# 480 guest columns of wq instead of 240, brought by SP and GpSimd

## The chip, the cores and the metric

The kernel runs on one core of one Trainium2 chip. The metric is device time in microseconds (us): the median of several runs of the whole program.

## The reference

One decode step (one token, batch 4) of a transformer block with adaptive layer norm: sliding window attention over a cache, then a gated feed-forward layer. All is float32.

```python
mod = (silu(c) @ w_mod).reshape(B, 6, 1, -1)           # sa, ca, ga, sb, cb, gb
h = layernorm(x) * (1 + ca) + sa                       # x: [4, 1, 512]
q = h @ wq                                             # wq: 512 x 4096, 32 heads of 128
# keys and values: the last 2048 positions of the cache, 8 heads, each shared by 4 query heads
o = softmax(q k^T / sqrt(128)) v
x = x + ga * (o @ wo)
h = layernorm(x) * (1 + cb) + sb
x = x + gb * ((silu(h @ w1) * (h @ w3)) @ w2)          # w1, w3: 512 x 1792, w2: 1792 x 512
```

## The kernel before

About 101 MB of weights, keys and values are loaded once, and nearly every load has 128 partitions, so that its rows are spread evenly over the 16 DMA engines. The big buffer `ring` has three `slots` of 16384 columns (64 KB a partition). `w_mod_a` (the modulation weights for sa and ca, with x and c) lands in the first 4128 columns of `slots[0]`, `wq` in `slots[1]`, and the cache of the eight groups (`kv[0]` to `kv[7]`, one per key head) goes round the slots: `kv[0]` in `slots[2]`, `kv[1]` in `slots[0]` when the modulation columns no longer need it, `kv[2]` in `slots[1]` when the queries no longer need wq, and so on. Later come `wo_mod`, `last_k_wo`, `last_v`, `wo`, `w1`, `w3` and `w2` (in four pieces). SP issues all loads but wq, which ACT issues.

Instructions are recorded by `do(engine, method, ...)` in program order (all of them at one source line, L59, in the profile). `Program` works out which earlier accesses overlap, and puts semaphore waits in front of an instruction; each engine and each queue goes through its own instructions in the order written. A wait on an engine is a wait for the latest of its instructions that touches the same place.

The start: `w_mod_a` and `wq` are loaded; constants are made on GpSimd (POOL in the profile) and VectorE (DVE); then layer norm, `mod_columns` (the modulation columns on TensorE, PE), `modulate`, which gives `h`, and `transposed`, which gives `hT`. Then the queries: wq is laid out so that `s_ps[half]` takes half of the heads; its four quarters of 32 partitions (i = 0 to 3) each sum four products (k = 0 to 3) of 512 columns. The loops are half, k, i, with i innermost.

**Guests.** The last 240 columns of wq's last quarter (half 1, i = 3, k = 3) aren't in the load of wq. Their 128 rows lie in another input, `guests`, 24 rows of 6 x 240 columns, and come by eight loads of SP, each of 3 partitions (4 apart), to the partitions 0 to 11 and 32 to 43 of `p_all`, over zeros. The matching rows of h come from six matmuls of `h` with a slice of the identity (`hp`, copied to `hg`), and six matmuls with `hg` and `guest` add the guests' share to the last 240 columns of the quarter.

Behind the queries come, for each group g, the scores, the softmax, the products with the values and the heads (`group`), and after `group(g)` the issue of `kv[g + 3]`. The end is the feed-forward layer, whose last pieces of w2 arrive last.

Of the kernel before, what the change touches and what calls it, by code (L numbers as in the profile page):

```python
# [11 lines left out]
NT = 4  # L12
# [1 line left out]
CHUNKS = [(c, j) for c in range(4) for j in range(4 if c < 2 else 3)]  # L14
NF = len(CHUNKS)
W2_CUTS = [0, 8, 11, 13, 14]
GUESTS = 240
GUEST_AT = [(0, 0, 12), (12, 0, 12), (24, 0, 8), (64, 0, 12), (76, 0, 12), (84, 4, 12)]
EPS = 1e-5
HALF = 8192  # L20

# [123 lines left out]
                nc.sync.sem_clear(done)  # L145


def block_kernel(nc, w_mod_a, wq, guests, kv_in, wo_mod, last_k_wo, last_v, wo, w1, w3, w2, out):

# [2 lines left out]
    do = Program(nc)  # L154

    def sb(name, *shape):
        return nc.alloc_sbuf_tensor(name, (P, *shape), F32).ap()
# [5 lines left out]
    slots = [ring[:, n * 2 * HALF : (n + 1) * 2 * HALF] for n in range(3)]  # L163
# [6 lines left out]
    def bank():  # L170
        turn[0] += 1
        return banks[turn[0] % 2]

    def load(dst, src, cuts=(0, 1), queue="sync"):
        step = src.shape[1] // cuts[-1]
        for lo, hi in zip(cuts[:-1], cuts[1:]):
            do(queue, "dma_start", dst[:, lo * step : hi * step], src[:, lo * step : hi * step])
        return dst[:, : src.shape[1]]
# [9 lines left out]
    wq_t = load(slots[1], wq, queue="scalar")  # L188
    do("scalar", "preload_act_table_set", "natural_log_exp_and_others")
    kv = [None] * G  # L190
# [4 lines left out]
    ident = shifted[:, 4:]  # L195
    do("gpsimd", "memset", shifted, 0.0)
    do("gpsimd", "affine_select", ident, ident, compare_op=ALU.not_equal, fill=1.0, base=0, pattern=[[-1, P]], channel_multiplier=1)

    p_all = sb("p_sb", NT * 512)
    do("gpsimd", "memset", p_all[:44], 0.0)  # L200
    guest = p_all[:44, : 6 * GUESTS]
    for m in range(2):
        for c in range(4):
            do("sync", "dma_start", guest[32 * m + c : 32 * m + 12 : 4], guests[12 * m + c : 12 * m + 12 : 4])
    kv[0] = load(slots[2], kv_in[0])
    sc = sb("sc", 4, 32)
    do("gpsimd", "memset", sc, 0.0)
# [11 lines left out]
    spread = sb("spread", 32)  # L219
# [19 lines left out]
    e = sb("e", 16)  # L239
# [5 lines left out]
    xc, sq, h = (sb(n, P) for n in ("xc", "sq", "h"))  # L245
    ss, ln, r0, ve, a, r = (sb(n, 1) for n in ("ss", "ln", "r0", "ve", "a", "r"))
# [19 lines left out]
    def transposed(name):  # L266
        hp = bank()[:, :P]
        do("tensor", "transpose", hp, h, ident)
        hT = sb(name, 4, 32)
        do("vector", "tensor_copy", hT.rearrange("p j i -> p (j i)"), hp)  # L270
        return hT
# [21 lines left out]
    do("vector", "tensor_scalar_add", mod_a[:, P:], mod_a[:, P:], 1.0)  # L293
    modulate(mod_a[:, P:], mod_a[:, :P])
    hT = transposed("hT")
    kv[1] = load(slots[0], kv_in[1])


    hg = p_all[:44, 6 * GUESTS :][:, : 6 * 32]
    hp = bank()[:44, : 6 * 32]  # L300
    for n, (at, _, _) in enumerate(GUEST_AT):
        do("tensor", "matmul", hp[:, 32 * n : 32 * n + 32], h[:, at : at + 44], ident[:, 96:], start=True, stop=True)
    do("vector", "tensor_copy", hg, hp)

    work = sb("work", 512)
    for half in range(2):
        qp = s_ps[half]
        for k in range(4):
            for i in range(4):
                at = ((half * 4 + i) * 4 + k) * 512  # L310
                n = min(512, 16384 - GUESTS - at)
                if n < 512:
                    for c in range(6):
                        do("tensor", "matmul", qp[96:, n:], hg[:, 32 * c : 32 * c + 32], guest[:, c * GUESTS : (c + 1) * GUESTS], start=False, stop=False)
                do("tensor", "matmul", qp[32 * i : 32 * i + 32, :n], hT[:, k, :], wq_t[:, at : at + n], start=(k == 0), stop=(k == 3))
    for half in range(2):
        do("scalar", "mul", work, s_ps[half], DH**-0.5)
        qtp = bank()
# [2 lines left out]
        for i in range(R):  # L321
            src = qtp[:, i * P : (i + 1) * P].rearrange("p (g q) -> p g q", g=4)[:, :, ::8]
# [13 lines left out]
    p_sb = [p_all[:, t * 512 : (t + 1) * 512] for t in range(NT)]  # L336
# [132 lines left out]
    for n in range(W2_CUTS[1]):  # L469
        i = n % 4  # L470
# [22 lines left out]
def _layout(i):  # L493
    import numpy as np

    def a(t):
        return np.ascontiguousarray(t)

    k = i["A_k_cache"][:, :, SK - W :, :].reshape(B, G, NT, 512, DH)
    v = i["A_v_cache"][:, :, SK - W :, :].reshape(B, G, NT, NC, P, DH)  # L500
    wm = i["w_mod"].reshape(4, P, 6, 4, P)
    xc = np.concatenate([i[n].reshape(B, 4, P).transpose(2, 1, 0).reshape(P, 16) for n in ("A_x", "c")], 1)
    w2 = i["B_w2"].reshape(14, P, D)
    wq = a(i["A_wq"].reshape(4, P, G, 512).transpose(1, 2, 0, 3)).reshape(P, 16384)
    guests = np.zeros((2, 12, 6, GUESTS), np.float32)
    for n, (at, lo, hi) in enumerate(GUEST_AT):
        for m in range(2):
            guests[m, lo:hi, n] = wq[at + 32 * m + lo : at + 32 * m + hi, 16384 - GUESTS :]
    wo = a(i["A_wo"].reshape(2, 4, R, P, D).transpose(0, 3, 1, 2, 4)).reshape(2, P, 8192)
    kv = np.concatenate([k.transpose(1, 4, 2, 0, 3).reshape(G, P, 8192), v.transpose(1, 4, 2, 0, 3, 5).reshape(G, P, 8192)], 2)  # L510
    return {
        "w_mod_a": np.concatenate([a(wm[:, :, :2].transpose(1, 0, 3, 2, 4)).reshape(P, 4096), xc], 1),
        "wq": a(wq[:, : 16384 - GUESTS]),
        "guests": guests.reshape(24, 6 * GUESTS),
        "kv_in": kv[: G - 1],
        "wo_mod": np.concatenate([wo[0], a(wm[:, :, 2:].transpose(1, 0, 3, 2, 4)).reshape(P, 8192)], 1),
        "last_k_wo": np.concatenate([kv[G - 1, :, :8192], wo[1, :, :4096]], 1),
        "last_v": a(kv[G - 1, :, 8192:]),
        "wo": a(wo[1, :, 4096:]),
        "w1": a(i["B_w1"].reshape(4, P, FF).transpose(1, 0, 2)).reshape(P, 4 * FF),  # L520
        "w3": a(i["B_w3"].reshape(4, P, FF).transpose(1, 0, 2)).reshape(P, 4 * FF),
        "w2": a(np.stack([w2[4 * j + c] for c, j in CHUNKS], 1)).reshape(P, NF * D),
    }
# [15 lines left out]
```

## Time and profile before

| | |
|---|---|
| runs | 242.0 us median of 3 (241.97 to 242.18) |
| profiled execution | span 240.8 us from the first to the last instruction; the page gives no other time for it |
| busy | PE 148.7 us (62%), weight loads 54.2 (22%), DVE 56.3 (23%), ACT 24.1 (10%), POOL 4.5 (2%) |
| DMA | 101.39 MB in 2937 packets, mean 421 GB/s |
| granted clock of TensorE | 0.865 on average |

The page shows one execution. Its queues q1 and q10 are those of SP and ACT, q8 and q14 fetch instructions. A view in windows gives busy time, granted clock, the mean busy share of the 16 DMA engines and GB/s for chosen stretches; a packet is counted by its start, so that a share in a short stretch can be over 1. The chain is the work that ended last, followed back from the last instruction.

### The profile page before, as it was taken

The numbers are of one execution on the slowest core, as the hardware profiler recorded it, in microseconds if no ns is written. First come the engines' busy times: TensorE is split into PE (matmuls) and PEld (weight loads), VectorE is DVE, ScalarE is ACT, GpSimd is POOL, SyncE is SP. The second block draws the span as 40 slices with busy tenths as digits, with TensorE's granted clock in tenths as the row PEclk, the third lists the DMA queues.
The fourth block names the chain that finished last, engine by engine and source line by source line (L and its number), as shares of the span: only waits on it lengthen the run. The fifth ranks groups of instructions, "written<-read, shape, count | busy, mean of one in ns | idle before, by whom it ended". The sixth has DMA issues, their size and how long they took to land.

```text
span 240.8 us, 2502 instructions
## 1 busy us (share of the span) xinstructions
PE 148.7 (62%) x1113; PEld 54.2 (22%) x1113; DVE 56.3 (23%) x141; ACT 24.1 (10%) x36; POOL 4.5 (2%) x12
## 2 busy tenths in 40 slices
PE   0000169982984962944867576667399719965876
PEld 0000133322322212201312222221042202422333
DVE  5000231034152024123132133130313104113210
ACT  2000000003003003001100300300200001320100
POOL 7000000000000000000000000000000000000000
PEclk9999997997696798879797799795759968995899
DMA  8999999999999999999999999999999999999994
GB/s 305 434 444 455 424 425 446 416 446 414 457 395 468 403 459 414 449 425 446 425 446 427 435 435 435 435 427 446 425 446 425 411 419 430 386 444 443 401 413 162
DMA packets 2937, 101.39 MB, mean 421 GB/s; under 512 B 472, under 2 KB 472, under 8 KB 880
## 3 DMA queue, kind: packets, MB, share of 16 engines
q1 hardware_dynamic: 2784, 92.99, 89.8%
q10 hardware_dynamic: 144, 8.27, 8.0%
q8 instruction: 8, 0.13, 0.2%
q14 instruction: 1, 0.01, 0.0%
HBM read 101.22 MB, written 0.03 MB: 420 GB/s over the span
## 4 chain that ended last, share of the span: by engine, by line
DMA 60%; PE 31%; DVE 5%; ACT 3%; issue 1%; ACTq 0%
DMA ring<-kv_in 33%; DMA ring<-w 16%; PE s_ps L59 14%; DMA ring<-w_mod_a 11%; PE bank L59 9%; PE o_ps L59 6%; DVE nm L59 3%; ACT p_sb L59 3%; PE a_ps L59 1%; DVE mod_a L59 0%; ACT work L59 0%; DVE p_sb L59 0%; DVE e L59 0%; DVE h L59 0%; DVE sq L59 0%
## 5 line engine op out<-in xcount | busy, mean ns | idle before, releaser
L59 PE MATMUL s_ps<-ring,qT 128*32 128x512 f32 x256 | 36.5, 722 | 20.3 <-DMA ring<-kv_in 13.3
L59 PE MATMUL bank<-ident,p_sb 128*128 128x128 f32 (+1 forms) x136 | 27.7, 353 | 30.8 <-ACT p_sb L59 30.7
L59 PE MATMUL o_ps<-ring,pT 128*16 128x512 f32 x256 | 38.4, 707 | 0.1
L59 PEld LDWEIGHTS bank<-ident,p_sb 128*128 128x128 f32 (+1 forms) x136 | 19.8, 178 | 52.5 <-ACT p_sb L59 31.7
L59 ACT ACTIVATE p_sb<-s_ps,nm 128x2048 f32<-128x2048 f32 (+1 forms) x11 | 16.5, 1501 | 139.7 <-DVE oT L59 104.1
L59 DVE TENSOR_REDUCE nm<-s_ps 128x1 f32<-128x2048 f32 x7 | 16.0, 2292 | 32.5 <-PE s_ps L59 32.5
L59 DVE COPY pT<-bank 128x64 f32<-128x64 f32 x32 | 7.2, 225 | 57.0 <-PE bank L59 57.0
L59 PEld LDWEIGHTS s_ps<-ring,qT 128*32 128x32 f32 x256 | 8.7, 129 | 46.9 <-issue 20.1
L59 PE MATMUL bank<-ident,xs 128*128 128x128 f32 x1 | 0.5, 476 | 27.8 <-POOL xs L59 27.8
L59 PE MATMUL s_ps<-ring,h2T 128*32 128x512 f32 (+1 forms) x64 | 9.0, 657 | 2.3 <-DMA ring<-w 2.3
L59 PE MATMUL s_ps<-ring,hT 128*32 128x512 f32 (+1 forms) x64 | 9.4, 705 | 0.0
L59 PEld LDWEIGHTS o_ps<-ring,pT 128*16 128x16 f32 x256 | 5.4, 99 | 11.9 <-issue 9.0
L59 DVE SCALAR_TENSOR_TENSOR o_own<-o_ps,rl,own 128x512 f32<-128x512 f32 x7 | 5.3, 751 | 11.1 <-PE o_ps L59 11.1
L59 PE MATMUL a_ps<-ring,oT 128*4 128x512 f32 x64 | 7.4, 592 | 0.0
L59 DVE TENSOR_REDUCE o_sum<-o_own 128x128 f32<-128x512 f32 x7 | 7.2, 1034 | 0.2
L59 PE MATMUL bank<-ring,sc 128*32 128x256 f32 (+1 forms) x64 | 6.9, 587 | 0.0
L59 PEld LDWEIGHTS bank<-ident,xs 128*128 128x128 f32 x1 | 0.2, 183 | 27.8 <-POOL xs L59 27.8
L59 DVE TENSOR_SCALAR e<-e 128x16 f32<-128x16 f32 x1 | 0.2, 175 | 23.3 <-ACT e L59 23.3
L59 DVE COPY qT<-bank 128x64 f32<-128x64 f32 x8 | 2.2, 280 | 12.4 <-PE bank L59 12.0
L59 DVE TENSOR_REDUCE mx<-s_ps 128x1 f32<-128x512 f32 x4 | 2.8, 692 | 9.0 <-PE s_ps L59 9.0
L59 PEld LDWEIGHTS s_ps<-ring,h2T 128*32 128x32 f32 x64 | 2.6, 130 | 7.3 <-issue 4.4
L59 PE MATMUL s_ps<-ring,hidT 128*32 128x64 f32 (+1 forms) x112 | 3.6, 274 | 0.3 <-DVE hidT L59 0.3
(97 smaller groups left out, 63.7 us busy)
## 6 DMA issues: line engine op xcount, KB each, us to landing
ring<-wq ACTq DMA_DIRECT2D x1, 8072.0 KB, 26.9
ring<-w SPq DMA_DIRECT2D x2, 3584.0 KB, 37.9
ring<-last_k_wo SPq DMA_DIRECT2D x1, 6144.0 KB, 30.1
ring<-last_v SPq DMA_DIRECT2D x1, 4096.0 KB, 39.5
ring<-w_mod_a SPq DMA_DIRECT2D x1, 2064.0 KB, 26.7
ring<-wo SPq DMA_DIRECT2D x1, 2048.0 KB, 41.8
ring<-w SPq DMA_DIRECT2D x1, 2048.0 KB, 43.1
ring<-w SPq DMA_DIRECT2D x1, 768.0 KB, 44.5
```

The source lines that it names most:

```text
L59: op = Op(engine, lambda: getattr(getattr(self.nc, engine), method)(*args, **kw), [])
```

## The change

- `GUESTS` is 480. wq's load is 240 columns narrower still, and the quarter's last product (k = 3) keeps 32 of its 512 columns in it.
- The guests lie on 76 partitions: 0 to 11 and 64 to 75, with zeros between. Their place is `slots[0]`, columns 4128 to 7008, behind `w_mod_a`. VectorE clears it (GpSimd cleared `p_all` before).
- They come in three loads whose two sides are shaped differently. `low`: 12 partitions of 2880 columns, issued by SP; its source has 3 rows of 4 runs. `high_a`: 4 partitions of 3 x 640 columns, from 3 rows of 4 runs, and `high_b`: 8 partitions of 2400 columns, from 2 rows of 4 runs, both issued by GpSimd. In front of these two GpSimd issues a small load of 8 x 2 x 8 elements of wq into `work`, which nothing reads.
- `hg` takes seven matmuls of up to 76 rows (six of 44 before) and two copies (one before).
- The queries are computed quarter by quarter: first half 1, i = 3, with the guests' six matmuls directly behind k = 0; then the other seven quarters, with k innermost.
- The issue of `kv[1]` stands behind that first quarter; before, it stood behind `hT`.

```diff
-GUESTS = 240
-GUEST_AT = [(0, 0, 12), (12, 0, 12), (24, 0, 8), (64, 0, 12), (76, 0, 12), (84, 4, 12)]
+GUESTS = 480
+GUEST_ROWS = 76
+LOW = [[(0, 12, 12 * n)] for n in range(5)] + [[(8, 12, 116), (0, 8, 60)]]
+HIGH = [(64 + 4 * (n == 0), 76, 12 * n) for n in range(5)]
...
-    p_all = sb("p_sb", NT * 512)
-    do("gpsimd", "memset", p_all[:44], 0.0)
-    guest = p_all[:44, : 6 * GUESTS]
-    for m in range(2):
-        for c in range(4):
-            do("sync", "dma_start", guest[32 * m + c : 32 * m + 12 : 4], guests[12 * m + c : 12 * m + 12 : 4])
+    guest = slots[0][:GUEST_ROWS, 4128 : 4128 + 6 * GUESTS]
+    do("vector", "memset", guest, 0.0)
+
+    def quads(queue, dst, src, runs):
+
+        step = dst.shape[-1]
+        src = src[:, : runs * step + runs * 16].rearrange("e (r n) -> e r n", r=runs)[:, :, :step]
+        do(queue, "dma_start", dst, src)
+
+    p_all, work = sb("p_sb", NT * 512), sb("work", 512)
+    quads("sync", guest[:12], low, 4)
+    do("gpsimd", "dma_start", work[:8, :32].rearrange("p (s n) -> p s n", s=2)[:, :, :8], wq[:8, :16].rearrange("p (s n) -> p s n", s=2))
+    quads("gpsimd", guest[64:68, GUESTS : 5 * GUESTS].rearrange("p (a n) -> p a n", a=3), high_a, 4)
+    quads("gpsimd", guest[68:, : 5 * GUESTS], high_b, 4)
     kv[0] = load(slots[2], kv_in[0])
...
     hT = transposed("hT")
-    kv[1] = load(slots[0], kv_in[1])
...
+    tall = [GUEST_ROWS] * 5 + [12]
+    for n, parts in enumerate(LOW):
+        for _, rows, at in parts:
+            rows = GUEST_ROWS if n < 5 else rows
+            do("tensor", "matmul", hp[:rows, 32 * n : 32 * n + 32], h[:, at : at + rows], ident[:, 96:], start=True, stop=True)
+    do("vector", "tensor_copy", hg[:, :160], hp[:, :160])
+    do("vector", "tensor_copy", hg[:12, 160:], hp[:12, 160:])
+
+    def queries(half, i, guests=False):
         qp = s_ps[half]
         for k in range(4):
...
+            at = ((half * 4 + i) * 4 + k) * 512
+            n = min(512, 16384 - GUESTS - at)
+            do("tensor", "matmul", qp[32 * i : 32 * i + 32, :n], hT[:, k, :], wq_t[:, at : at + n], start=(k == 0), stop=(k == 3))
+            if guests and k == 0:
+                for c in range(6):
+                    do("tensor", "matmul", qp[96:, 512 - GUESTS :], hg[: tall[c], 32 * c : 32 * c + 32], guest[: tall[c], c * GUESTS : (c + 1) * GUESTS], start=False, stop=False)
+
+    queries(1, 3, True)
+    kv[1] = load(slots[0], kv_in[1])
+    for half in range(2):
+        for i in range(4 - half):
+            queries(half, i)
...
+    def spread(rows, engines, runs):
+        apart = np.zeros((engines, runs, rows.size // engines // runs + 16), np.float32)
+        apart[:, :, :-16] = rows.reshape(engines, runs, -1)
+        return np.pad(apart.reshape(engines, -1), ((0, 0), (0, 16)))
...
+        "low": spread(guests[:12], 3, 4),
+        "high_a": spread(guests[64:68, GUESTS : 5 * GUESTS], 3, 4),
+        "high_b": spread(guests[68:, : 5 * GUESTS], 2, 4),
```

More of the change, by code (lines that the diff above doesn't have):

```diff
@@ L145, in emit, with block_kernel @@
                 nc.sync.sem_clear(done)
-def block_kernel(nc, w_mod_a, wq, guests, kv_in, wo_mod, last_k_wo, last_v, wo, w1, w3, w2, out):
+def block_kernel(nc, w_mod_a, wq, low, high_a, high_b, kv_in, wo_mod, last_k_wo, last_v, wo, w1, w3, w2, out):
     do = Program(nc)
@@ L295, in block_kernel @@
     hT = transposed("hT")
-    kv[1] = load(slots[0], kv_in[1])
[L299 to L306, printed above, removed]
+    hg = p_all[:GUEST_ROWS, : 6 * 32]
+    hp = bank()[:GUEST_ROWS, : 6 * 32]
+    tall = [GUEST_ROWS] * 5 + [12]
[6 more added lines that the diff above has]
+    def queries(half, i, guests=False):
         qp = s_ps[half]
         for k in range(4):
[L309 to L315, printed above, removed]
+            at = ((half * 4 + i) * 4 + k) * 512
[9 more added lines that the diff above has]
+            queries(half, i)
     for half in range(2):
@@ L504, in _layout @@
     wq = a(i["A_wq"].reshape(4, P, G, 512).transpose(1, 2, 0, 3)).reshape(P, 16384)
[L505 to L508, printed above, removed]
+    guests = np.zeros((GUEST_ROWS, 6, GUESTS), np.float32)
+    for n, parts in enumerate(LOW):
+        for lo, hi, at in parts + HIGH[n : n + 1]:
+            guests[lo:hi, n] = wq[at + lo : at + hi, 16384 - GUESTS :]
+    guests = guests.reshape(GUEST_ROWS, 6 * GUESTS)
+    def spread(rows, engines, runs):
+        apart = np.zeros((engines, runs, rows.size // engines // runs + 16), np.float32)
+        apart[:, :, :-16] = rows.reshape(engines, runs, -1)
+        return np.pad(apart.reshape(engines, -1), ((0, 0), (0, 16)))
     wo = a(i["A_wo"].reshape(2, 4, R, P, D).transpose(0, 3, 1, 2, 4)).reshape(2, P, 8192)
@@ L513, in _layout @@
         "wq": a(wq[:, : 16384 - GUESTS]),
-        "guests": guests.reshape(24, 6 * GUESTS),
+        "low": spread(guests[:12], 3, 4),
+        "high_a": spread(guests[64:68, GUESTS : 5 * GUESTS], 3, 4),
+        "high_b": spread(guests[68:, : 5 * GUESTS], 2, 4),
         "kv_in": kv[: G - 1],
```

## The prediction

> **What bounds the kernel now.** I read the page's head, its queues and chain first.
>
> ```profile
> span 240.8 us, 2502 instructions
> q1 hardware_dynamic: 2784, 92.99, 89.8%
> q10 hardware_dynamic: 144, 8.27, 8.0%
> q8 instruction: 8, 0.13, 0.2%
> DMA 60%; PE 31%; DVE 5%; ACT 3%; issue 1%; ACTq 0%
> ```
>
> SP's and ACT's queues keep the 16 DMA engines busy for 97.8% of the span. PE's 31% of the chain lies beside transfers, save for the end. The time is therefore the time of the DMA engine that finishes last, plus the tail behind it. Next, stretches of the windows view (columns: stretch, its length, PE busy, clock, DMA share, GB/s):
>
> ```profile
> 33.50:36.90 3.40, 1.54 (x29) 1.00 1.29 559
> 36.90:40.30 3.40, 3.40 (x20) 0.50 0.84 366
> 40.30:45.40 5.10, 5.10 (x50) 1.00 0.97 414
> 67.40:190.00 122.60, 83.87 (x554) 0.83 1.00 433
> 236.10:236.40 0.30, 0.30 (x8) 1.00 0.76 307
> 236.80:237.30 0.50, 0.50 (x48) 1.00 0.71 274
> 237.30:237.70 0.40, 0.36 (x27) 1.00 0.40 149
> 237.70:238.10 0.40, 0.40 (x44) 1.00 0.00 0
> ```
>
> 433 GB/s at share 1.00 is 27.1 KB/us for each engine. At 236.1 only 0.76 of the engines (12 of 16) still work, at 236.8 0.71 (11), and the last stop near 237.7. So four or five engines end 1.3 us or more ahead; the other eleven set the end. Why eleven, two DMA views say: a stretch with an instruction fetch (43.5 to 44.6), and bytes started per slice of 0.0475 us from 26.3 on.
>
> ```profile
> q8 instruction: 1, 0.02, 5.3%
> GB/s 1623 1501 1380 2760 2760 1744 1380 1380 0 243 121 0 0 0 1623 2881 0 0 0 364 0 0 0 121 243 0 0 0 243 121 0 0 0 364 0 0 0 1380 2759 0
> ```
>
> The fetch holds one engine for 5.3% of 16 x 1.1 us = 0.93 us. In the second row the bursts of 1380 are packets of 65.5 KB, the first of kv[0]. Three of them start at 28.1, behind the small packets of the guests (121 each), 1.8 us later than the first ones at 26.3. Three engines with guests and the eight fetches of q8 make the eleven, though one fetch may fall on an engine that is done.
>
> **Part 1: bytes.** Guests go from 240 to 480 columns, so wq loses 240 x 4 B in each of 128 rows: 7.7 KB an engine, **-0.28 us** on all 16. SP's part was 24 rows of 5,760 B and becomes 12 rows of 11,520 B: the same 138 KB. If it stays on three engines it costs them the same 1.7 us, and they too gain 0.28. POOL's part is 4 x 7,680 + 8 x 9,600 = 107.5 KB. With the first on one engine and the second on two, those three get 30.7 or 38.4 KB, +1.13 or +1.41 us. Net of wq that is +0.85 to +1.13, which an engine with 1.3 us to spare absorbs. Bounds of this part: -0.28 where the three are idle ones; +1.13 where one of them is already late. The trace names no engines.
>
> The Trainium skill, "DMA: Bandwidth & Descriptors", section "Why a DMA increments its semaphore by 16 and not by 1", says that a DMA uses the largest count up to 16 that divides the slowest dimension of both sides, from engine 0 up on SP, and from a cursor that moves round on POOL. By it low takes 3 engines, the small load 8 (it moves the cursor), high_a 1, high_b 2. The burst of three at 28.1 agrees for SP; no POOL load is in this trace.
>
> **Part 2: the start.** Timeline, up to 28 us:
>
> ```profile
> 1.41 1.80 POOL L59 MEMSET p_sb<- 44x2048 f32 x1
> 1.51 0.48 DVE L59 MEMSET a_ps<- 128x512 f32 x1
> 3.23 5.67 SPq L59 DMA_DIRECT2D p_sb<-guests  x8
> 8.95 0.42 SPq L59 DMA_DIRECT2D ring<-kv_in  x1
> 27.55 0.21 POOL L59 COPY xs<-ring 128x16 f32<-128x16 f32 x1 [22.52 <-DMA ring<-w_mod_a]
> ```
>
> The new DVE memset has 2880 columns: 2880/512 x 0.48 = 2.7 us, and ends near 3.5. low's issue waits for it, as the guests waited for POOL until 3.23. One issue of about 0.7 replaces eight (5.67), so kv[0] is queued near 4.3 instead of 8.95; the engines are full with w_mod_a and wq until 26.3, so this brings nothing. DVE's other small steps of the start wait 2.7 us; nothing needs them before w_mod_a lands (27.4). POOL loses its 1.80 memset and gets three issues, with its other memsets behind them. No row shows a POOL issue; SP's take 0.42 to 0.7, and POOL has about 20 idle us before 27.55, so I put 0, covered by that; without the cover each us would delay the whole start. Packets that POOL puts among w_mod_a's delay its landing: between -0.28 (wq alone) and +1.13. I take **+0.5**, the middle, since the last of 16 engines counts.
>
> **Part 3: the moved load.** This is where the change can lose. kv[1] goes to slots[0], where the guests now lie, so SP issues it behind the last guest matmul; until now it waited for the modulation columns alone. Pieces of the chain, timelines of SP and PE, and two groups (busy us, mean ns):
>
> ```profile
> 0.73 26.68 DMA ring<-w_mod_a
> 30.30 3.81 PE bank L59 x34
> 36.85 11.81 PE s_ps L59 x76
> 34.19 0.33 SPq L59 DMA_DIRECT2D ring<-kv_in  x1
> 48.70 0.33 SPq L59 DMA_DIRECT2D ring<-kv_in  x1
> 50.60 3.65 PE s_ps L59 x32
> 67.41 38.51 DMA ring<-kv_in
> 40.65 3.62 PE L59 MATMUL s_ps<-ring,hT 128*32 128x512 f32 x32
> 45.48 2.61 PE L59 MATMUL s_ps<-p_sb 44*32 44x240 f32 x12
> L59 PE MATMUL bank<-ident,h 128*44 128x32 f32 x12 | 0.7, 208 | 0.0
> L59 PE MATMUL s_ps<-p_sb 44*32 44x240 f32 x12 | 2.6, 364 | 0.0
> ```
>
> Each float32 call is two passes. Guests of 240 columns, all for one quarter of PE, follow one another each 2.61/12 = 0.21 us at full clock; of 480 columns 0.42, at clock 0.50 0.84. A pass of 512 takes 0.43 (32 in 3.62, four abreast) or 0.86. The queries start at 36.85; +0.5 from part 2, +0.1 for one more call of hg (0.7/6): 37.45. Two passes of k = 0 at half clock: 39.15. Until 40.3 1.4 guest passes; the other 10.6 at full clock take 4.4: 44.7. With +0.2 until PE reports (a pass lasts 0.36, 0.15 more than the spacing) and +0.1 to SP (34.11 to 34.19 today) the issue is at **45.0**, 10.8 later than now. When would bytes follow, and when must they? GB/s rows of 0.5 to 2.5, of 238 to 240.8, and of 45 to 47, each in 40 slices:
>
> ```profile
> GB/s 0 0 0 0 0 0 0 0 0 0 0 0 0 0 0 0 0 0 0 0 0 0 0 0 330 1651 330 660 1321 0 660 0 0 0 0 0 330 0 0 0
> 239.34 0.34 SPq L59 DMA_DIRECT2D out<-p_sb  x1
> GB/s 0 0 0 0 0 0 0 0 0 0 0 0 0 0 0 0 0 0 0 0 0 0 0 0 0 0 0 0 0 0 0 106 209 132 22 0 0 0 0 0
> GB/s 3932 0 0 0 0 0 0 0 0 0 0 0 0 2622 1311 2622 2622 1311 0 1311 0 0 0 0 0 0 1311 2622 0 0 0 0 0 0 0 0 0 0 0 0
> ```
>
> First bytes come 0.83 us after an issue (239.34 to 240.17) or 0.97 (0.73 to 1.70): 45.83 to 45.97. Engines without guests begin kv[1] at 45.65 now, and would be free at 45.37. Their kv[1] starts +0.18 to +0.32 from today's, not -0.28. Those hit by a fetch later carry this to the end: **+0.25**, instead of -0.28. Bounds: -0.28 (full clock throughout: 37.45 + 0.86 + 12 x 0.42 + 0.3 = 43.7, in time) and +1.0 (half clock 1.7 us longer, or w_mod_a at +1.13). The half-clock stretch lies where PE idled shortly before, and may fall elsewhere in another execution.
>
> **Part 4: queries quarter by quarter.** The order was k outside, quarters inside, and four quarters ran abreast (32 passes in 3.62 us are 0.11 each). Now the eight passes of a quarter stand together. If PE still overlaps quarters, the last queries end near 45 + 1.7 + 56 x 0.11 = 53, 4 us later than today; two abreast, near 59. kv[2], behind kv[1] on SP, waits for it (48.70 today) and must start when kv[1] ends, near 65 (45.65 + 19.4); so this costs 0. Compute starts late and catches up: a group's loads take 8.4 MB/433 GB/s = 19.4 us, its compute less (from 50.6 to 67.4 for the first), and kv[3], issued at 67.41 today, has the 19.4 us of kv[2] in front of it.
>
> **Sum.** -0.28 from wq, +0.53 from the late kv[1]: +0.25 at the last engine in the likeliest case. The tail moves with it. The page gives the profiled execution's span alone, 240.8; this makes it 241.05. The runs' median of 242.0 holds 1.2 more around the span, so **242.2**.
>
> **The rivals.**
> kv[1] in time (full clock, or a small delay of w_mod_a): -0.28, 241.7. For it: 1.0 us is all that is missing. Against it: the 0.50 row lies just there.
> POOL's loads meet late engines: +1.13, 243.1; it decides as soon as one of the three is among the eleven of 16 that end late. Against it: four to five idle ones exist. For it: nothing in the trace says that POOL reaches them. This is also how the change would fail to do what it says.
> kv[1] much too late: w_mod_a at +1.1 or the half clock longer; issue at 45.6 or later, +0.6 to +1.0, so 242.6 to 243.0.
> One quarter after another: PE runs the passes strictly as written; 56 x 0.43 = 24 us, the queries end near 71, kv[2] starts 6 us after 65, 248. It decides when the queries end after 64. Against it: if the two passes of a call had to run in turn before the next call began, at most two quarters would be abreast, and 32 passes would take about 6.9 us, not 3.62.
> The Trainium skill, "TensorE: Matmul & The Clock Gate", section "Part 3: Packing small matmuls — row/col tiling", has matmuls start and end strictly in program order, which speaks for this last case; the 3.62 us speak against it here.
>
> **How the numbers follow.** Runs of this kernel spread by 0.1% (241.97 to 242.18); 0.2% (0.48 us) is about what a measurement tells from no change. Late kv[1] (-0.1 to +0.45): 0.34, same. In time: 0.26, same. POOL on late engines: 0.20, slower. Much too late: 0.10, slower. One after another: 0.06, slower. Faster by 0.5 us or more: 0.04, for which no row speaks, since the bytes taken from every engine are worth 0.28. Same 0.60, slower 0.36. The range reaches from just under the in-time case, 241.6, to the POOL case, 243.2; above it lie the last 6% and little else. The likeliest case's own range is 241.9 to 242.5.
>
> **What the profile would show.** SP's issue of kv[1] near 45.0 (in time: before 44.4), and the first bytes of kv[1] near 45.9 where 45.65 stands. In the last 1.5 us the DMA share above 0.71: 14 of 16 engines, if POOL's loads fell on idle ones; a lower share and a later end, if not. Twelve guest passes of 480 columns behind two passes of k = 0. Last queries near 53, not 71; w_mod_a at about 27.9. The prediction is wrong if kv[1]'s issue lies before 44 or beyond 46, if the three engines of POOL are late ones, or if the queries end after 64.

## The result, and the profile after

The changed kernel takes **251.0 us** (median of 5, 250.81 to 251.16) where the kernel before, run beside it, takes 242.18 (241.97 to 242.48): a ratio of 1.036 (95% interval 1.035 to 1.037). 242.2 was predicted, with a range to 243.2. The change is slower by 8.8 us. Here and below, the ratios leave out single executions that came out far above the fastest of their kernel (483.3 us in own_place_11, 248.3 in own_place_no_pool, the two longer ones of kv0_in_four).

The DMA share in 40 slices (tenths) of before, then the page of the changed kernel: span, the DMA share in slices of 6.24 us, POOL's queue (q0), and the chain.

```profile
DMA  8999999999999999999999999999999999999994
...
span 249.6 us, 2500 instructions
...
DMA  9999999149799998989989899999999999899993
...
q0 software_dynamic: 224, 0.11, 0.2%
...
PE 44%; DMA 42%; DVE 6%; ACT 5%; issue 2%; ACTq 0%
```

The span grew by 8.8 us, as much as the time. Before, every slice but the first and the last of the DMA row read 9. Now slices 7 and 8, counted from 0 (43.7 to 56.2 us), read 1 and 4. On the chain DMA falls from 60% to 42% and PE rises from 31% to 44%, since transfers wait for PE. The windows view says when (stretch, length, five engines' busy time, clock, DMA share, GB/s), and an answer of 40 slices of 0.1625 us from 53.5 on shows how the bytes come back:

```profile
26.50:46.00 19.50, 11.98 (x59) 5.09 (x60) 4.19 (x18) 0.68 (x3) 0.21 (x1) 1.00 0.96 413
46.00:48.00 2.00, 2.00 (x4) 0.47 (x3) 0.00 (x0) 0.00 (x0) 0.00 (x0) 1.00 0.00 0
48.00:53.50 5.50, 5.50 (x8) 0.74 (x7) 0.00 (x0) 0.00 (x0) 0.00 (x0) 1.00 0.00 0
...
GB/s 0 4033 1613 807 0 0 0 0 0 0 0 0 0 0 0 0 0 0 403 807 2016 2420 807 0 0 0 0 0 0 0 0 0 0 403 1210 1714 2016 807 0 0
```

(GB/s are booked where a packet starts.) No packet starts between 46.0 and 53.5; those that began earlier run out. kv[1]'s first bytes come at 53.66 (slice 1) where 45.65 stood before: 8.0 us. The second round starts 17 to 20 slices, 2.8 to 3.2 us, behind the first, the third only about 15, 2.4 us, behind the second: the first packets after the idle stretch take about 0.6 us more. 8.0 + 0.6 = 8.6 of the 8.8. So nearly all of the loss has come about by kv[1]'s first packets. Why kv[1] is so late, the timelines of POOL, SP and PE show:

```profile
1.79 0.73 POOL L61 DMA_DIRECT2D work<-wq  x1 [0.32 <-issue]
4.18 0.69 POOL L61 DMA_DIRECT2D ring<-high_a  x1 [1.65 <-DVE ring L61]
4.86 0.58 POOL L61 DMA_DIRECT2D ring<-high_b  x1
...
38.16 1.06 PE L61 MATMUL s_ps<-ring,hT 128*32 128x512 f32 x1
39.02 1.06 PE L61 MATMUL s_ps<-ring,hT 128*32 128x512 f32 x1
42.77 9.91 PE L61 MATMUL s_ps<-ring,p_sb 76*32 76x480 f32 x12 [2.69 <-issue]
52.61 17.13 PE L61 MATMUL s_ps<-ring,hT 128*32 128x512 f32 x62
...
52.71 0.33 SPq L61 DMA_DIRECT2D ring<-kv_in  x1
```

PE ends the two passes of k = 0 at 40.08 and stands idle for 2.69 us. "issue" as releaser says only that the view knows none; the DMA view has it (issue to landing in us, and, in answers for 8 to 11 and for 30.3 to 41 us, packets of each queue):

```profile
ring<-high_b POOLq DMA_DIRECT2D x1, 75.0 KB, 37.8
ring<-high_a POOLq DMA_DIRECT2D x1, 30.0 KB, 26.1
...
q10 hardware_dynamic: 16, 1.02, 78.4%
q1 hardware_dynamic: 16, 0.26, 20.9%
q0 software_dynamic: 16, 0.00, 0.5%
...
q1 hardware_dynamic: 72, 4.72, 101.7%
q0 software_dynamic: 60, 0.08, 2.0%
```

high_b, issued at 4.86, lands 37.8 us later, at 42.7, just before the guests start. `low`, SP's part, isn't what they wait for: its 12 packets have all started by 27.7. In 3 us each of 16 engines has moved one packet of ACT's queue (wq, 64 KB), one of SP's (w_mod_a, 16 KB) and one of POOL's. Later, beside kv[0]'s packets of 64 KB, it is again about one to one (72 and 60). A POOL load thus advances by about one packet per round of the other queues, however small its packets are. (A round is the time in which an engine has moved one packet of each queue.) And POOL's three loads are 224 packets, 14 for each of 16 engines, though only 22 of those carry data (8 of 64 bytes, 6 of 5,120 and 8 of 9,600): the others are of 4 or 8 bytes. high_b's last data start at 39.5; it counts as landed one round later, behind packets of 4 bytes.

The Trainium skill has the rule ("DMA: Bandwidth & Descriptors", section "Queues, rings and completion order"): an engine goes round the queues that have work and drains one packet of each. The trace agrees, one packet of each in 3 us; the prediction did not use it.

Then the twelve guest passes start 0.80 us apart or a little more (9.84 us from 42.77 to 52.61), not 0.42, and only behind them is kv[1] issued. I call this half clock, but that is read from the passes and not from the clock column, which shows 1.00 in all rows above. The column is no witness here. Weight loads of the query passes behind the guests, in the timeline:

```profile
56.03 0.18 PEld L61 LDWEIGHTS s_ps<-ring,hT 128*32 128x32 f32 x2 [0.67 <-issue]
...
58.24 0.14 PEld L61 LDWEIGHTS s_ps<-ring,hT 128*32 128x32 f32 x2 [0.29 <-issue]
```

Until 56.9 these come every 0.85 us, from 57.4 on every 0.43, at a column of 1.00 on both sides. So the passes became twice as fast at about 57, 4.4 us behind the start of the query passes, and the column shows nothing of it.

### The profile page after: what moved, and what is told of

Read it like the earlier page. It is cut to its first block, busy times and chain, and to the rows that moved or that the text cites. A ratio compares the mean times of both kernels' runs of the same rounds, so it can differ in the third digit from the quotient of the medians.

```text
span 249.6 us, 2500 instructions
## 1 busy us (share of the span) xinstructions
PE 164.0 (66%) x1115; PEld 58.3 (23%) x1115; DVE 59.3 (24%) x143; ACT 24.1 (10%) x36; POOL 4.6 (2%) x14
## 4 chain that ended last, share of the span: by engine, by line
PE 44%; DMA 42%; DVE 6%; ACT 5%; issue 2%; ACTq 0%
PE s_ps L61 21%; DMA ring<-w 15%; DMA ring<-wo_mod 15%; PE bank L61 12%; DMA ring<-w_mod_a 11%; PE o_ps L61 10%; DVE nm L61 5%; ACT p_sb L61 4%; PE a_ps L61 1%; DVE mod_a L61 0%; ACT work L61 0%; DVE p_sb L61 0%; DVE e L61 0%; DVE oT L61 0%; DVE h L61 0%
## 5 line engine op out<-in xcount | busy, mean ns | idle before, releaser
L61 PE MATMUL bank<-ident,p_sb 128*128 128x128 f32 (+1 forms) x136 | 28.5, 361 | 30.8 <-ACT p_sb L61 30.7
L61 PE MATMUL s_ps<-ring,qT 128*32 128x512 f32 x256 | 32.7, 657 | 9.8 <-DMA ring<-last_k_wo 7.0
L61 PEld LDWEIGHTS bank<-ident,p_sb 128*128 128x128 f32 (+1 forms) x136 | 20.5, 184 | 52.9 <-ACT p_sb L61 31.7
L61 PE MATMUL s_ps<-ring,hT 128*32 128x512 f32 (+1 forms) x64 | 19.0, 651 | 0.0
L61 PE MATMUL s_ps<-ring,p_sb 76*32 76x480 f32 (+1 forms) x12 | 9.9, 1004 | 2.7 <-issue 2.7
L61 PE MATMUL s_ps<-ring,h2T 128*32 128x512 f32 (+1 forms) x64 | 9.6, 694 | 1.4 <-DMA ring<-w 1.0
L61 PEld LDWEIGHTS s_ps<-ring,hT 128*32 128x32 f32 x64 | 4.8, 120 | 13.2 <-issue 13.2
## 6 DMA issues: line engine op xcount, KB each, us to landing
ring<-w SPq DMA_DIRECT2D x1, 768.0 KB, 44.5
```

The lines of the kernel that those rows point to most:

```text
L61: op = Op(engine, lambda: getattr(getattr(self.nc, engine), method)(*args, **kw), [])
```

## The experiments

Theory from here on: the change made kv[1]'s load wait for the guests, the guests wait for POOL's last load, that lands at 42.7 because of the rounds, and the guests then run at half clock; each us by which kv[1] is late is a us of the end. Rivals: the order quarter after quarter costs it; POOL's traffic by itself costs it.

**quarter_order: the new order alone.**

```
 (before)
-        for k in range(4):
-            for i in range(4):
+        for i in range(4):
+            for k in range(4):
```

> The kernel before, with only the order of the query products changed: k inside, quarters outside. Theory: two quarters abreast instead of four, the last queries end near 54 instead of 48.7, kv[2] is issued then, but isn't due before about 65: 242.2, within 0.3. Rival (this order is what costs): +5 us or more, 247 to 251.

Measured 242.13 us, ratio 0.9995 (0.9985 to 1.0005). Timelines of PE and SP:

```profile
37.48 16.66 PE L59 MATMUL s_ps<-ring,hT 128*32 128x512 f32 x62
...
57.29 0.33 SPq L59 DMA_DIRECT2D ring<-kv_in  x1
```

The 62 passes of 512 columns take 16.66 us where 62 in the old order take 7.94 (in late_kv1, below), so only two quarters run abreast (at the same time); kv[2] is issued at 57.29 instead of 48.70, and it costs nothing, since kv[1]'s bytes flow until 65. The order alone costs nothing.

**late_kv1: the late load alone.**

```
 (before)
-    kv[1] = load(slots[0], kv_in[1])
     ... all query products
+    kv[1] = load(slots[0], kv_in[1])    # and this load waits for the last product
```

> The kernel before, with one wait added: SP issues kv[1] only behind the last query product (near 48.7 instead of 34.2). Guests, order and places stay as before. Theory (an engine that idles before kv[1] never catches up): first bytes near 49.6 instead of 45.65, and the first packets after an idle stretch take 3.1 us instead of 2.42, together +4.5: 246.7 (245.8 to 247). Rival (compute has slack for the later groups, so a late kv[1] is given back): 242.2 to 243.

Measured 247.01 us (245.61 to 247.50), ratio 1.019 (1.016 to 1.022): 4.8 us. The pieces of the chain in order of time:

```profile
37.76 11.01 PE s_ps L59 x76
48.77 0.02 issue
48.79 23.15 DMA ring<-kv_in
71.93 0.04 issue
71.98 6.19 PE s_ps L59 x32
```

Its timeline of PE has the queries in the old order:

```profile
37.69 7.94 PE L59 MATMUL s_ps<-ring,hT 128*32 128x512 f32 x62
```

kv[1] was issued at 48.79, first bytes came at 49.7, 4.1 behind the 45.65 of before; with 0.6 for the first packets 4.7. A stop of all 16 engines is not given back. No guests, place or order were touched here.

**own_place: the coupling and the new order taken away.** The 480 guests and their three loads stay, but lie in a tile of their own; kv[1] is issued behind the modulation again and the products are in the order of before.

```
 (changed)
-    guest = slots[0][:GUEST_ROWS, 4128 : 4128 + 6 * GUESTS]
+    big = sb("p_sb", NT * 512 + 1024)            # also p_all, o_own, mod_b
+    guest = big[:GUEST_ROWS, : 6 * GUESTS]
...
     hT = transposed("hT")
+    kv[1] = load(slots[0], kv_in[1])
...
-    queries(1, 3, True)
-    kv[1] = load(slots[0], kv_in[1])
```

> 480 guests in three loads as in the change, but in a place of their own (p_sb, o_own and mod_b become views of one tile), so that kv[1] is issued behind the modulation as before; the query products are in the order before the change, k outside, the guests ahead of the last product. Theory (the coupling of kv[1] to the guests is the whole loss): kv[1] issued near 34.5, guests at 44 to 50 at full clock, queries end near 51, kv[2] in time; wq's 0.28 us gained: 241.9, within 0.3. Rival (POOL's traffic costs by itself): 243 or more. Rival (480 columns of one quarter are too much PE time): the queries end after 65 and the time goes over 245.

**pool_loads_alone: POOL's traffic alone.** The kernel before with POOL's three loads into columns that nobody reads.

```
 (before)
+    do("gpsimd", "dma_start", work[:8, ...], wq[:8, ...])
+    quads("gpsimd", big[64:68, 480:2400]..., high_a, 4)
+    quads("gpsimd", big[68:76, :2400], high_b, 4)
     kv[0] = load(slots[2], kv_in[0])
```

> The kernel before, with its 240 guests, and beside them POOL's three loads of the change (38 KB on one engine, 77 KB on two, the small one) into columns that nobody reads; p_sb, o_own and mod_b become views of one tile to make room. Theory: the loads land near 12, 30 and 43 us as in the changed kernel, nothing waits for them, and they fall on engines that end early: 242.2 to 242.5. Rival (POOL's packets, with their fillers on engines that carry no data, cost by themselves, or fall on late engines): +1.1 or more, 243.3 to 244.

own_place measured 243.37 us, ratio 1.0057 (1.0035 to 1.0079), where 241.9 was expected: 7.6 of the 8.8 us are gone with the coupling and the new order together; own_place_quarters, below, puts the order back. pool_loads_alone measured 243.95, ratio 1.0070 (1.0051 to 1.0089), where 242.2 to 242.5 was expected: in both the rival was right, POOL's loads do cost 1.2 to 1.8 us when nothing else stops the engines. The ends of the loads, in the windows view (DMA share, GB/s last), of own_place and behind the dots of pool_loads_alone:

```profile
237.50:238.00 0.50, 0.50 (x15) 0.20 (x10) 0.00 (x0) 0.00 (x0) 0.00 (x0) 1.00 0.23 90
238.00:238.50 0.50, 0.50 (x46) 0.50 (x42) 0.00 (x0) 0.32 (x1) 0.00 (x0) 1.00 0.12 45
238.50:239.00 0.50, 0.46 (x33) 0.30 (x25) 0.00 (x0) 0.27 (x1) 0.00 (x0) 1.00 0.10 37
239.00:239.40 0.40, 0.40 (x40) 0.40 (x36) 0.00 (x0) 0.00 (x0) 0.00 (x0) 1.00 0.00 0
...
238.00:238.50 0.50, 0.50 (x36) 0.43 (x32) 0.00 (x0) 0.18 (x1) 0.00 (x0) 1.00 0.12 49
238.50:239.00 0.50, 0.47 (x36) 0.30 (x27) 0.00 (x0) 0.41 (x1) 0.00 (x0) 1.00 0.14 53
```

Before, the share is 0.00 from 237.7 on. In both kernels some 0.12, two engines of 16, work a good 1 us longer than that. The next runs show whose bytes make them late.

**own_place_no_pool, no_pool_again, own_place_small_only: which part of POOL's traffic.** The first two leave out POOL's three loads, the third only high_a and high_b; the last quarter's product lacks those rows.

> The kernel own_place without POOL's three loads; the guests' rows 64 to 75 stay zero, so that part of the last quarter's product is left out. Everything else, the twelve guest passes too, is as in own_place. Theory (own_place's loss of 1.2 us comes from POOL's packets alone): eleven engines end late as in the kernel before, all with 7.7 KB less: 241.9. Rival (the 480-column guests, their memset or SP's new load cost it): 243.4.

> own_place_no_pool once more (the high rows left out), for its profile. It measured 242.07, where wq's 7.7 KB less in each engine should have made 241.9 of the 242.18 of before. Theory A (the gain lasts to the end of the loads and the measurement is too coarse for it): last load landed near 237.9, where 238.14 stands before, span 240.6. Theory B (a fetch or another delay falls on an engine that is late already): last load landed at 238.1 or later, with the earliest engines at 236.25 instead of 236.53.

> The kernel own_place with only the first of POOL's three loads, the small one of 512 bytes; the high rows stay zero, so that part of the last quarter's product is left out. Theory (the 38 KB that three engines carry for POOL put a second delay on them): without these bytes 242.07, as without any POOL load. Rival (POOL's queue costs by its packets of 4 and 8 bytes and its turns, whatever it carries): 242.7 or more.

Measured 242.07, ratio 0.9997 (0.9988 to 1.0005); 242.03, ratio 1.0000 (0.9990 to 1.0010); and 241.98, ratio 0.9991 (0.9982 to 1.0000). Without the high loads the 1.3 us are gone, with the small load's 32 packets still there: it is the high loads that cost. That it is their bytes fits the size (38.4 KB are 1.41 us) and the two late engines; their own packets of a few bytes were not tried alone. Does wq's 0.28 us reach the end? The windows at the end of before, then the first line and the windows of no_pool_again:

```profile
237.00:237.50 0.50, 0.47 (x35) 0.30 (x25) 0.00 (x0) 0.44 (x1) 0.00 (x0) 1.00 0.68 262
237.50:238.00 0.50, 0.50 (x36) 0.50 (x40) 0.00 (x0) 0.00 (x0) 0.00 (x0) 1.00 0.08 29
...
span 240.6 us, 2497 instructions
...
237.00:237.50 0.50, 0.47 (x36) 0.33 (x28) 0.00 (x0) 0.12 (x1) 0.00 (x0) 1.00 0.23 86
237.50:238.00 0.50, 0.50 (x49) 0.50 (x41) 0.00 (x0) 0.00 (x0) 0.00 (x0) 1.00 0.00 0
```

The loads end earlier, and the span is 0.2 shorter than before, own_place_small_only's (240.4) 0.4: about what was expected. The times can't tell it from nothing, since every interval reaches 1.000.

**own_place_11, own_place_13, own_place_5, own_place_3: other engines for POOL's rows.** The small load, whose only use is to move the place where POOL's next load begins, covers another number of partitions.

```
 (own_place)
-    do("gpsimd", "dma_start", work[:8, ...], wq[:8, ...])
+    do("gpsimd", "dma_start", work[:11, ...], wq[:11, ...])    # and 13, 5, 3
```

> The kernel own_place with one size changed: the small load of POOL covers 11 partitions instead of 8. By the Trainium skill ("DMA: Bandwidth & Descriptors", section "Why a DMA increments its semaphore by 16 and not by 1") a POOL load starts at a cursor that the load before it moved by its count, so the high loads go three engines further. Theory (own_place lost 1.2 us because two of the three engines that carry POOL's high rows are also held up by an instruction fetch, two delays on one engine): the three engines change, and the time changes with them: 241.9 where none of the three is hit by a fetch, 243.4 where one is. Rival (POOL's packets cost wherever they go): 243.4, as own_place.

> The kernel own_place with POOL's small load over 13 partitions instead of 8, so that the high loads go five engines further. Same theory and rival: 241.9 where none of the three engines is hit by a fetch, 243.4 where one is; rival 243.4 in any case. With three places tried (8, 11, 13), the theory wants at least one of them near 241.9.

> The kernel own_place with POOL's small load over 5 partitions instead of 8: the high loads go three engines back. With 11 and 13 partitions they also made every kv[0] packet between 30 and 42 us longer (2.6 to 2.8 us instead of 2.42), which with 8 they did not. Theory (what counts is which engines carry them): the time differs from 243.4 again, 241.9 if none of the three is hit by an instruction fetch later, 243.4 to 243.7 if one or two are, one more us if kv[0]'s packets are stretched as well. Rival (the place does not matter): 243.4.

> The kernel own_place with POOL's small load over 3 partitions: the high loads go five engines back. Same theory and rival as own_place_5: 241.9 on free engines, 243.4 to 243.7 with a fetch on one of them, one more us with stretched packets; rival 243.4.

Measured 245.07 (11), 244.64 (13), 245.05 (5) and 244.73 (3); ratios 1.0115 (1.0098 to 1.0132), 1.0103 (1.0088 to 1.0118), 1.0115 (1.0102 to 1.0128) and 1.0127 (1.0102 to 1.0153). The place matters, but every other place is worse than 8, and none is free: the theory wanted at least one near 241.9. Of the difference the windows view shows one part: while high_b is under way, all transfers are slower. The stretch from 30 to 42 us of own_place, then of own_place_13:

```profile
30.00:42.00 12.00, 9.55 (x69) 4.81 (x73) 2.96 (x13) 0.46 (x2) 0.00 (x0) 1.00 0.99 427
...
30.00:42.00 12.00, 9.44 (x71) 4.90 (x75) 3.03 (x13) 0.46 (x2) 0.00 (x0) 1.00 1.01 400
```

427 and 400 GB/s at the same share; kv[0]'s packets take up to 2.8 us instead of 2.42. Why is open. Whether the two late engines of own_place were hit by an instruction fetch as well, these runs don't show: the trace names no engines.

**kv0_in_four: high_b earlier.** Smaller packets beside POOL's.

```
 (changed)
-    kv[0] = load(slots[2], kv_in[0])
+    kv[0] = load(slots[2], kv_in[0], (0, 1, 2, 3, 4))
```

> The changed kernel, with kv[0] loaded by four instructions (packets of 16 KB instead of 64 KB). Theory (POOL's last load lands at 42.7 us because each of its 13 turns waits behind one packet of every other queue): eight turns pass by 26 us as now, the last five at about 0.6 us each, so that high_b lands near 30 instead of 42.68; the guests then start near 37.5. If their passes stay at 0.80 us each (half clock, whatever PE did before) they end near 48, kv[1] is issued near 48 instead of 52.7, time 246.4 (246 to 247). If the clock is half only because PE stood idle from 39.9 to 42.7, it is full from about 41, kv[1] is issued near 44.5, time 243. Rival (the order quarter after quarter is what costs): high_b's landing doesn't matter, time stays at 251.0.

Four runs scatter from 243.7 to 248.0 us (median 247.08, ratio 1.011 (1.006 to 1.016)); the profiled execution is the one of 247.8, so what follows is read for its mechanism and not for its time. Its DMA view and timelines:

```profile
ring<-high_b POOLq DMA_DIRECT2D x1, 75.0 KB, 27.0
...
38.90 1.06 PE L61 MATMUL s_ps<-ring,hT 128*32 128x512 f32 x1
39.75 9.94 PE L61 MATMUL s_ps<-ring,p_sb 76*32 76x480 f32 x12
49.62 16.62 PE L61 MATMUL s_ps<-ring,hT 128*32 128x512 f32 x61
```

high_b lands 10.8 us earlier, at about 32: the rounds set the landing, as expected. PE doesn't wait any more, the guests start right behind k = 0 at 39.75, and still take 9.87 us. So the half clock doesn't come of PE's idle time before them. The guests end 3.0 us earlier than in the changed kernel, and the profiled execution is 3.1 shorter (247.8 against 250.9). What the 243.7 did differently is not shown; a clock that rose earlier would fit it.

**filler: PE kept at work on all quarters.**

```
 (changed)
             if guests and k == 0:
+                for f in range(16):
+                    do("tensor", "matmul", a_ps[32 * (f % 4) : ...], hT[:, f % 4, :], wq_t[:, 512 * f : ...], ...)
                 for c in range(6):
```

> The changed kernel with 16 products more (32 passes on all four quarters of PE, into a_ps, whose content is discarded), put between the first query product and the guests, so that PE works while it waits for high_b. Theory A (passes on one quarter never bring the clock up, four abreast do, as in the kernel before from 40.3 on): the clock is full from about 41, the guests start near 42.8, take 0.42 us each instead of 0.80, kv[1] is issued near 48: 246.3. Theory B (480-column passes take 0.80 us by themselves, or the clock falls back as soon as one quarter works alone): kv[1] near 52.7, 251.0. In both, high_b lands near 42.7.

Measured 247.44 us (246.53 to 248.42), ratio 1.021 (1.017 to 1.025); the profiled execution is one of 248.3. Timelines of PE and SP:

```profile
38.90 5.76 PE L61 MATMUL a_ps<-ring,hT 128*32 128x512 f32 x29
44.50 5.11 PE L61 MATMUL s_ps<-ring,p_sb 76*32 76x480 f32 x12
...
49.64 0.33 SPq L61 DMA_DIRECT2D ring<-kv_in  x1
```

With 32 passes more in front, the same twelve guest passes take 5.04 us (0.42 each) instead of 9.84: theory A is right that passes four abreast bring the clock up, and 0.80 is no property of a guest pass. The fillers ran until 44.5, 1.8 longer than high_b, so kv[1] is issued at 49.64, 3.1 earlier than in the changed kernel, not 4.7; the median fell by 3.6, the profiled execution by 2.6.

**own_place_quarters: something else late.** own_place with the changed kernel's order; kv[1] early.

```
 (own_place)
-    half, k, i: guests ahead of the last product
+    queries(1, 3, True)
+    for half in range(2):
+        for i in range(4 - half):
+            queries(half, i)
```

> The kernel own_place with the order of the changed kernel: the last quarter first, with the guests behind its first product, and then quarter by quarter. kv[1] is issued early (near 34.3) in both. Theory (the order costs only through what waits behind it): PE waits for high_b until 42.7, the guests run at half clock until 52.6, the last queries end near 69.6, kv[2] is issued there and should be flowing when kv[1] ends near 66: the engines idle 4 to 5 us, 243.4 + 4.5 = 247.9. Rival (kv[2] has slack enough, only kv[1]'s place cost the changed kernel): 243.4.

Measured 248.32 us (247.66 to 248.74), ratio 1.025 (1.024 to 1.027). Windows around the end of kv[1], and SP's timeline:

```profile
64.00:67.00 3.00, 3.00 (x18) 0.89 (x16) 0.00 (x0) 0.60 (x1) 0.00 (x0) 1.00 0.10 44
67.00:70.00 3.00, 3.00 (x13) 0.89 (x10) 0.00 (x0) 0.00 (x0) 0.00 (x0) 1.00 0.00 0
...
69.73 0.33 SPq L61 DMA_DIRECT2D ring<-kv_in  x1
```

Now kv[2], issued at 69.73 behind the last query, is the late one: the engines run dry between 65 and 67 and stand until 70.6, and 5 us are lost though kv[1] was in time. The order that costs nothing in quarter_order costs 5 us here, because wait and half clock have moved the queries' end from 57 to 69.7, past the point at which kv[1]'s bytes run out.

## Why the prediction was wrong

**What held.** The bound was named rightly: the time is that of the transfers, and a late kv[1] is carried to the end. The rival "kv[1] much too late" was the mechanism; it had a chance of 0.10, and +0.6 to +1.0 us where +8.6 came. Bytes follow kv[1]'s issue by 0.95 us (0.83 to 0.97). Part 2's issues on POOL (0.58 to 0.73 us each) lie beside idle time as put, and w_mod_a lands at 27.66, 0.25 later (0.5 put). Part 4 holds in that two quarters run abreast, and in the changed kernel this costs nothing. All three of the prediction's signs of being wrong came: kv[1]'s issue at 52.71, beyond 46; the queries' end at 69.7, beyond 64, by the wait and the half clock; and late engines with POOL's rows (own_place).

**Part 2, the step that failed first.** It priced POOL's issues and asked what their packets do to w_mod_a. It never asked when POOL's own loads land: it put 0 for the issues and +0.5 for w_mod_a, and Part 3 let the guests start right behind k = 0, at 39.15. Their bytes are little (107 KB), but they travel in 14 packets per engine, about one per round of 2.4 us (a 64 KB packet of kv[0]) to 3 us (one of wq and one of w_mod_a). As an estimate, 14 rounds of 2.4 to 3 us from 4.86 on end at 39 to 47. high_b landed at 42.7, with the guests, and so kv[1], behind it.

**Part 3, the step that failed second.** "The other 10.6 at full clock" took a row of before (0.50 until 40.3, then 1.00) as a matter of time. The runs tie it to the work: there, four quarters were abreast. Passes on one quarter ran 9.84 us without becoming faster, here and, without idle time before them, in kv0_in_four, while filler's passes over four quarters brought the full clock, and so did the query passes behind the guests, two abreast, by 57. The Trainium skill ("TensorE: Matmul & The Clock Gate", section "Part 1: The HAM clock gate (the "warmup" mystery)") has the clock rise after some 3.4 to 4 us of sustained work; by that too the guests should have been fast from 42 or 46 on, and the runs disagree for work that fills one quarter.

These two steps make nearly all of the miss in kv[1]'s issue, predicted at 45.0 and measured at 52.71: 0.7 from the queries' start and k = 0 (39.9 instead of 39.15), 2.9 of waiting for high_b (until 42.77), 4.3 from the passes (9.84 instead of 5.55), less 0.2 for the reports that were put too high: 7.7 us.

**Part 1 failed as well, unseen in the result.** "Which an engine with 1.3 us to spare absorbs" is wrong: own_place and pool_loads_alone lose 1.2 and 1.8 us by POOL's loads, as the rival "POOL's loads meet late engines" had it (243.1, against 243.37 and 243.95). In the changed kernel it isn't seen, since 8.6 of the 8.8 us are accounted for without it; that it hides in the stretch in which all 16 engines stand still is likely, not shown. wq's -0.28 agrees with the spans (-0.2 and -0.4) and is too small for the medians (-0.06 to -0.2). So the change had nothing to gain even with its guests in a place of their own: 243.4 with POOL's rows, 242.0 when they are left out, 242.18 before.

## What to carry to other kernels

When a load moves to another queue, price its landing, not only its issue: count its packets on one engine, multiply by the round that the largest packets of the other queues make, and compare with the first instruction that waits. Before a buffer is shared with an early load, write down the latest moment at which that load may start, and what every waiting step on the way there depends on. A clock seen in a stretch belongs to the work of that stretch and of the one before it; passes that fill one quarter of PE and begin at half clock are to be reckoned at half clock to their end, until a trace shows otherwise.

## What the runs showed of the hardware

- A POOL load of 75 KB, issued at 4.86 us, landed 37.8 us later beside packets of 64 KB, and 27.0 later when kv[0] came in packets of 16 KB; POOL's three loads made 224 packets, 14 for each of 16 engines, 22 of them with data.
- Twelve passes of 480 columns on one quarter of PE, begun at half clock, took 9.84 us and did not become faster on the way; behind 32 passes over four quarters they took 5.04. The clock column of the windows showed 1.00 in both.
- Passes are four abreast when neighbours are of different quarters, two abreast when the eight passes of a quarter stand together: 62 passes in 7.9 and in 16.7 us.
- The first packets of 64 KB behind a stop of all engines (6 us in the changed kernel) took about 3.1 us instead of 2.42. Whether the stop does it, or that all 16 engines then start within 0.4 us, no run shows.
- With POOL's high loads begun at other places, everything moved more slowly between 30 and 42 us: 400 GB/s instead of 427 in own_place_13. No run explains it.
